# From unit 24 on: q, k and P turned in 32x32 blocks by VectorE, with a scratch in DRAM, in place of TensorE transposes

## The chip, the cores and the metric

The kernel runs on one core of a Trainium2 chip. The metric is the device time of one execution in microseconds (us), median of several runs. TensorE is PE (its weight loads PEld), VectorE DVE, ScalarE ACT, GpSimd POOL, SyncE SP; SP computes nothing here and issues all DMAs of the windowed path.

## The reference

Attention with 4 batches, 8 heads, 768 positions and head size 64, a local window of 96 keys, 8 global keys and a linear distance bias, then a feed-forward layer with a rational activation:

```python
scores = scale * np.matmul(q, k.transpose(0, 1, 3, 2))     # 4 x 8 x 768 x 768
keep = is_global | is_local                                # key < 8, or 0 <= row - key < 96
scores = np.where(keep, scores - slope * dist, -1e9)
a = softmax(scores)
x = np.matmul(a, v)        # laid out as 3072 tokens x 512
h = x @ w_in               # 512 -> 2048
g = (a0 + a1*h + a2*h**2 + a3*h**3) / (1 + |b0|*|h| + |b1|*h**2 + 1e-6)
out = g @ w_out            # 2048 -> 512, float32
```

## The kernel before, in words

Attention is cut into 96 units. A unit `u` is one pair of heads (4 pairs) in one tile of 128 rows (6 tiles in a batch, 24 in all): tile `u // 4`, pair `u % 4`. `unit(u)` also gives `i`, the tile's place in its batch. A tile with `i = 0` sees one block of keys, a later one its own block, the block before and the 8 global keys. The feed-forward is cut into 96 steps `f` (eight for each chunk of 256 tokens), each of 24 matmuls of 256 columns (`st_ffn1`, L312) and 12 of 512 columns (`st_ffn2`, L408), with the activation between them (`st_ew1`, `st_poly`, `st_sum`, `st_ew3`, `st_ew4`, `st_high`, `st_low`) on ACT, POOL and DVE. The weights and x are split in a high and a low part, so that three fast matmuls stand for one.

Units below 24 (`RAWQ`) work alone. From unit 24 on two units, here called a duo (`u` even and `u + 1`, four heads), are worked together, and four units (a tile) share one product P times v:

- `st_load` (L176): q and k of four heads come into `nat` (2 buffers).
- `st_split` (L482): a DMA copies `nat` to `sp`, typed for the fast matmul.
- `st_qkT` (L488): PE turns q and k of the duo, 4 transposes (L502) into PSUM (`tk`); `st_qkE` (L523): ACT copies them to `qT` (with the scale of the head) and `kT`.
- `st_score` (L558): scores in pieces of 32 queries, so that only the needed keys are computed; the key axis of a piece is ordered as a ring of 32-key blocks, own and previous block mixed (L580).
- `st_max`, `st_soft`, `st_total`, `st_norm` (L596 to L632): the masked maximum on DVE, the exponential on ACT, the scaling by the row's sum on POOL.
- `st_raw` (L634): a DMA copies P (`pr`) to `raws`, typed for the fast matmul (from unit 28).
- `st_pT` (L648): PE turns P, 2 transposes (L655) and for `i > 0` one for the global keys (L658); `st_pTE` (L664): DVE separates the ring into own and previous block by a multiplication with `block` (L676) and copies the global rows (L679).
- `st_pv` (L684): 16 matmuls for four units (L696), then `st_x` and `st_xl` split the result into the x of the feed-forward.

The order of the work has two parts. `LEAD` (L50) is a list of words that sets the order on all engines up to unit 29 (`T24` is `st_pT(24)`, `sp24` is `st_split(24)`, `BL` is `st_blocks`). Behind it a loop over `t` (L793) emits the steps, PE in that order; for ACT, DVE, POOL and SP a scheduler picks among the ready instructions by priority (`PRI`, L93), and the order so found is fixed in the program. At run time each engine takes its own instructions strictly in order and waits at each for its semaphores. The two halves of `st_ffn2(f)` come two loop steps behind `st_ffn1(f)`.

Of the kernel before, what the change touches and what calls it, by code (L numbers as in the profile page):

```python
# [17 lines left out]
P = 128  # L18
# [6 lines left out]
RAW = 28  # L25
RAWQ = 24
# [6 lines left out]
RAWS = 3  # L33
WK = P + 2 * G
PITCH = P + KB
# [57 lines left out]
PRI = dict(load=0, score=50, soft=100, ffn1a=150, qkT=200, pv=250, qkE=300, x=350, split=400, ew3=450, norm=500, raw=501,  # L93
# [51 lines left out]
def tile_kernel(ctx: ExitStack, tc: tile.TileContext, q, k, v, n_global, n_local,  # L145
# [336 lines left out]
    def st_split(u):  # L482
        if u >= RAWQ and u % 2 == 0:
            s = pl.att.tile([P, 2, 4, D], FR, tag="rawq", name=f"sp{u}", bufs=2)
            nc.sync.dma_start(out=s.bitcast(F32), in_=nat[u // 2])
            sp[u] = s

    def st_qkT(u):  # L488
        p = unit(u)[2]
        if u < RAWQ:  # L490
# [6 lines left out]
        elif u % 2 == 0:  # L497
            s = sp.pop(u)
            tk = pl.ps_t.tile([P, 2, 2, P], FR, tag="t", name=f"tk{u}")
            for y in range(2):  # L500
                for z in range(2):
                    nc.tensor.transpose(out=tk[:, y, z, :], in_=s[:, z, 2 * y:2 * y + 2].rearrange("p a d -> p (a d)"),  # L502
                                        identity=ident_r)
            tqk[u] = tk.bitcast(F32)


    def st_blocks():
        for p in range(NPAIR):
            for x in range(2):
                nc.gpsimd.memset(qsc[x * D:(x + 1) * D, p:p + 1], float(2.0 ** (2 * p + x - 2)))  # L510
        nc.gpsimd.tensor_copy(out=near[:, 0:G], in_=masks[:, 0, 0:G])
        nc.gpsimd.tensor_copy(out=near[:, G + P:], in_=masks[:, 0, 0:G])
        nc.gpsimd.tensor_copy(out=near[:, G:2 * G], in_=masks[:, 1, 0:G])
        nc.vector.tensor_tensor(out=near[:, 2 * G:G + P], in0=masks[:, 0, G:], in1=masks[:, 1, G:], op=ALU.max)
        nc.gpsimd.memset(raws2[:, :, :, G + P:].bitcast(F32), 0.0)
        nc.gpsimd.memset(block, 1.0)
        for w in range(2):
            sign = -1 if w else 1
            nc.gpsimd.affine_select(out=block[:, w, 0], in_=block[:, w, 0], pattern=[[sign * KB, P // KB], [0, KB]],
                                    base=-KB if w else KB - 1, channel_multiplier=-sign,  # L520
                                    compare_op=ALU.is_ge, fill=0.0)

    def st_qkE(u):  # L523
        c, t, p, b, i = unit(u)
        if u >= RAWQ:
            if u % 2 == 0:
                tk = tqk.pop(u)
                qTs[u] = qT = pl.att.tile([P, 2, P], F32, tag="qT", name=f"qT{u}")
                for y in range(2):
                    nc.scalar.activation(out=qT[:, y], in_=tk[:, y, 0], func=AF.Copy, scale=qsc[:, p + y:p + y + 1])  # L530
                nc.scalar.copy(out=kT[:, p:p + 2, i % 2, G:G + P], in_=tk[:, :, 1])
            return
# [11 lines left out]
    def st_kG(u):  # L544
        c, t, p, b, i = unit(u)
        if i:
            return
        if u < RAWQ:
            nc.gpsimd.tensor_copy(out=kG32[:, p, :], in_=k32[p][:, 0, 0:G])
        elif u % 2 == 0:  # L550
            for e in (0, G + P):
                nc.gpsimd.tensor_copy(out=kT[:, p:p + 2, :, e:e + G],
                                      in_=kT[:, p:p + 2, 0:1, G:2 * G].broadcast_to([P, 2, 2, G]))

    def first_of(x):
        return 0 if x else G

    def st_score(u):  # L558
        c, t, p, b, i = unit(u)
        if u < RAWQ:  # L560
# [9 lines left out]
        qT = qTs.pop(u)  # L570
        s_ps = [pl.ps_t.tile([P, 2, G + P], F32, tag="t", name=f"s{u}_{x}") for x in range(2)]
        for y in range(2):
            for part in range(2 if i else 1):
                for Q in range(P // KB - part):
                    for x in range(2):
                        first = first_of(x)
                        ends = (0, G + KB * (Q + 1) - first, G + P) if i else (G - first, G + P - first)
                        lo, hi = (0, G + P) if i and Q == P // KB - 1 else ends[part:part + 2]
                        own, qs = slice(x * D, (x + 1) * D), slice(Q * KB, (Q + 1) * KB)
                        nc.tensor.matmul(out=s_ps[x][qs, y, lo:hi], lhsT=qT[own, y, qs],  # L580
                                         rhs=kT[own, p + y, (i - part) % 2, first + lo:first + hi], start=True, stop=True)
# [3 lines left out]
    def st_kg(u):  # L585
        c, t, p, b, i = unit(u)
        if 1 <= i < NT - 1 and u < RAWQ:
            nc.gpsimd.tensor_copy(out=k32[p][:, i % 2, 0:G], in_=kG32[:, p, :])

    def cols_of(u, t, x):  # L590
        i = unit(u)[4]
        if u < RAWQ:
            return blocks_of(t, i)
        return t if i else t[:, G - first_of(x):][:, 0:P]

    def st_max(u):  # L596
        c, t, p, b, i = unit(u)
        s_ps = scores.pop(u)
        if u < RAWQ:
            mk = mask0 if i == 0 else masks[:, 0:2, :] if i % 2 else masks[:, 1:3, :]  # L600
            pr = pl.att.tile([P, 2, 2, P], F32, tag="prob", name=f"pr{u}")
        else:
            pr = pl.att.tile([P, 2 * PITCH], F32, tag="prob", name=f"pr{u}").rearrange("p (x w) -> p x w", x=2)[:, :, 0:G + P]
        st = stats[:, u % 4]
        for x in range(2):
            h = 2 * p + x
            if u >= RAWQ:
                mk = near[:, first_of(x):][:, 0:G + P] if i else mask0
            nc.vector.tensor_tensor_reduce(  # L609
                out=cols_of(u, pr[:, x], x), in0=cols_of(u, s_ps[:, x] if u < RAWQ else s_ps[x], x), in1=mk,  # L610
# [3 lines left out]
    def st_soft(u):  # L614
        pr, st = prob[u]
        for x in range(2):
            d = cols_of(u, pr[:, x], x)
# [9 lines left out]
    def st_norm(u):  # L627
        pr, st = prob[u]
        for x in range(2):
            d = cols_of(u, pr[:, x], x)  # L630
# [3 lines left out]
    def st_raw(u):  # L634
        if u < RAW:
            return
        pr = prob[u][0]
        raw = raws2[:, u % RAWS, :, 0:G + P]
        if unit(u)[4]:
            nc.sync.dma_start(out=raw.bitcast(F32), in_=pr)  # L640
        else:
            for x in range(2):
                nc.sync.dma_start(out=cols_of(u, raw[:, x].bitcast(F32), x), in_=cols_of(u, pr[:, x], x))
        prob[u] = (raw, None)
# [3 lines left out]
    def st_pT(u):  # L648
        i = unit(u)[4]
        pr, st = prob.pop(u)  # L650
        dt, eye = (FR, ident_r) if u >= RAW else (F32, ident)
        tps[u] = t_ps = pl.ps_t.tile([P, 2, 2, P] if u < RAWQ else [P, 3, P], dt, tag="t", name=f"tp{u}")
        if u >= RAWQ:
            for x in range(2):
                nc.tensor.transpose(out=t_ps[:, x], in_=pr[:, x, G - first_of(x):][:, 0:P], identity=eye)  # L655
            if i:
                ends = raws2[:, u % RAWS].rearrange("p x w -> p (x w)")[:, P:P + D]
                nc.tensor.transpose(out=t_ps[0:D, 2], in_=ends, identity=eye)  # L658
            return
        for x in range(2):  # L660
            for w in range(2 if i else 1):
                nc.tensor.transpose(out=t_ps[:, x, w, :], in_=pr[:, x, w, :], identity=eye)  # L662

    def st_pTE(u):  # L664
        i = unit(u)[4]
        pTs[u] = pT = pl.att.tile([P, 2, 2, P], F32, tag="pT", name=f"pT{u}", bufs=PTS)
        t_ps = tps.pop(u)
        t_ps = t_ps.bitcast(F32) if u >= RAW else t_ps
        copy = nc.scalar.copy if u < EARLY else nc.vector.tensor_copy
        if u < RAWQ:  # L670
# [361 lines left out]
```

## Time and profile before

| | us |
|---|---|
| median of 3 runs (lowest, highest) | 726.84 (724.93, 728.16) |
| the profiled execution | 725.79 |
| its span, first to last instruction | 723.8 |

| engine | busy, share of the span |
|---|---|
| PE | 700.3 us, 97% |
| DVE | 562.7 us, 78% |
| ACT | 552.7 us, 76% |
| POOL | 340.8 us, 47% |

The span is the time between the first and the last instruction in the trace; the execution's own time is 2.0 us longer. Busy times are unions of an engine's instructions. Matmuls overlap in the records, so what a matmul costs in a dense stretch is read from the start of one to the start of the next.

### The profile page before, as it was taken

Reading aid. Unit: us, or ns where it says so; the run is one execution under the profiler, and the core shown is the slowest. Engines: PE = TensorE matmul, PEld = TensorE weight load, DVE = VectorE, ACT = ScalarE, POOL = GpSimd, SP = SyncE. Lnnn points to the kernel's source line nnn. Section 1 sums busy time; section 2 is a strip of 40 time slices with the busy share of each in tenths; the row PEclk is TensorE's granted clock in tenths of the full one; section 3 lists DMA queues with packets and bytes.
Section 4 is the critical chain, followed back from the end, with each engine's and each line's share of the span. In section 5 each row is a group of like instructions: output and inputs, shape, how many; then the busy total and the mean of one; then the engine's idle time right before and its main releaser. Section 6 shows DMA issues by size and latency. Waiting matters only on the chain.

```text
span 723.8 us, 17630 instructions
## 1 busy us (share of the span) xinstructions
PE 700.3 (97%) x6515; PEld 602.1 (83%) x6515; DVE 562.7 (78%) x1419; ACT 552.7 (76%) x1302; POOL 340.8 (47%) x450
## 2 busy tenths in 40 slices
PE   5799999999999999999999999999999999999996
PEld 4577778768798888988888988888889888899995
DVE  6899999986976777877787877778687778777564
ACT  6899998867877867777776776877876867766774
POOL 2344646475445444455454454545445535444441
PEclk9999999999999999999999999999999999999998
DMA  8874446112322312323312322223222221100001
GB/s 196 254 223 128 147 140 174 39 44 74 99 67 76 98 54 81 100 62 89 104 47 77 104 62 77 92 73 89 89 61 77 90 62 54 54 19 1 30 1 35
DMA packets 110718, 62.29 MB, mean 86 GB/s; under 512 B 80672, under 2 KB 99616, under 8 KB 110624
## 3 DMA queue, kind: packets, MB, share of 16 engines
q1 hardware_dynamic: 110624, 61.07, 29.4%
q8 instruction: 54, 0.88, 0.5%
q14 instruction: 40, 0.33, 0.1%
HBM read 35.92 MB, written 6.29 MB: 58 GB/s over the span
## 4 chain that ended last, share of the span: by engine, by line
PE 85%; ACT 10%; DVE 2%; issue 1%; DMA 1%; SPq 1%; POOL 0%; ACTq 0%; POOLq 0%; DVEq 0%
PE acc L424 33%; PE h L330 32%; PE o L696 5%; PE s L580 3%; PE acc L420 3%; PE h L322 2%; ACT pr L618 2%; PE tk L502 2%; PE s L564 2%; PE tp L655 1%; DMA r<-in_moe_w_in_dram 1%; ACT qzero L537 1%; PE tp L662 1%; ACT r L261 1%; ACT fu L355 1%
## 5 line engine op out<-in xcount | busy, mean ns | idle before, releaser
L369 POOL TENSOR_TENSOR fa<-fa,fs 128x512 f32<-128x512 f32 (+1 forms) x86 | 110.3, 1282 | 234.4 <-ACT fs L357 226.9
L398 POOL TENSOR_TENSOR g<-fu,g 128x512 fp32r<-128x512 f32 x84 | 108.9, 1297 | 61.8 <-ACT g L395 54.8
L424 PE MATMUL acc<-wout_h,g 128*128 128x512 f32 x352 | 128.2, 408 | 0.7 <-POOL g L398 0.7
L355 ACT ACTIVATE fu<-h,coef 128x512 f32<-128x512 f32 x94 | 73.2, 778 | 69.7 <-PE h L330 69.5
L424 PE MATMUL acc<-h,g 128*128 128x512 f32 x336 | 121.4, 407 | 0.1
L385 DVE SCALAR_TENSOR_TENSOR fu<-fu,coef,q 128x512 f32<-128x512 f32 (+1 forms) x97 | 71.7, 739 | 57.8 <-ACT q L381 56.8
L330 PE MATMUL h<-xl,win_h 128*128 128x256 f32 x352 | 99.1, 282 | 0.7 <-DVE xl L735 0.6
L330 PE MATMUL h<-xh,win_h 128*128 128x256 f32 x352 | 99.6, 283 | 0.0
L330 PE MATMUL h<-xh,h 128*128 128x256 f32 x352 | 99.2, 282 | 0.0
L330 PE MATMUL h<-xl,h 128*128 128x256 f32 x352 | 98.2, 279 | 0.0
L395 ACT CAST g<-fu 128x512 fp32r<-128x512 f32 (+1 forms) x88 | 54.6, 620 | 49.1 <-DVE fu L387 49.0
L631 POOL TENSOR_SCALAR pr<-pr,stats 128x136 f32<-128x136 f32 (+2 forms) x170 | 65.9, 408 | 44.5 <-DVE stats L625 36.5
L380 ACT ACTIVATE fs<-fa,coef 128x512 f32<-128x512 f32 (+1 forms) x97 | 70.0, 722 | 21.3 <-POOL fa L369 19.8
L618 ACT ACTIVATE pr<-pr,stats 128x136 f32<-128x136 f32 (+2 forms) x192 | 80.5, 429 | 5.1 <-DVE stats L609 4.8
L364 DVE TENSOR_TENSOR fu<-fu,h 128x512 f32<-128x512 f32 (+1 forms) x97 | 65.8, 678 | 18.6 <-ACT fs L357 18.1
L424 PEld LDWEIGHTS acc<-wout_h,g 128*128 128x128 f32 x352 | 65.9, 188 | 15.2 <-issue 1.9
L424 PEld LDWEIGHTS acc<-h,g 128*128 128x128 f32 x336 | 62.9, 188 | 14.2 <-issue 1.7
L365 DVE SCALAR_TENSOR_TENSOR fu<-fu,coef,h 128x512 f32<-128x512 f32 (+1 forms) x97 | 71.8, 740 | 2.7
L386 DVE SCALAR_TENSOR_TENSOR q<-fa,coef,q 128x512 f32<-128x512 f32 (+1 forms) x97 | 72.2, 744 | 0.0
L330 PEld LDWEIGHTS h<-xl,win_h 128*128 128x128 f32 x352 | 66.2, 188 | 4.6 <-DVE xl L735 2.8
L387 DVE SCALAR_TENSOR_TENSOR fu<-q,fu 128x512 f32<-128x512 f32 (+1 forms) x97 | 66.5, 686 | 3.3
L330 PEld LDWEIGHTS h<-xh,win_h 128*128 128x128 f32 x352 | 66.2, 188 | 2.5 <-issue 0.5
(272 smaller groups left out, 1801.8 us busy)
## 6 DMA issues: line engine op xcount, KB each, us to landing
sp<-nat SPq DMA_DIRECT2D x36, 256.0 KB, 2.5
r<-in_moe_w_in_dram SPq DMA_DIRECT2D x16, 512.0 KB, 4.9
r<-in_moe_w_out_dram SPq DMA_DIRECT2D x16, 512.0 KB, 4.8
raws<-pr SPq DMA_DIRECT2D x60, 136.0 KB, 2.2
nat<-in_q_dram SPq DMA_DIRECT2D x48, 128.0 KB, 2.4
nat<-in_k_dram SPq DMA_DIRECT2D x48, 128.0 KB, 2.6
vt<-in_v_dram SPq DMA_DIRECT2D x48, 128.0 KB, 2.7
out_dram<-o SPq DMA_DIRECT2D x18, 256.0 KB, 2.2
```

The lines of the kernel that those rows point to most:

```text
L330: nc.tensor.matmul(out=h_of(f, y), lhsT=w[:, fs], rhs=x[:, ct, :], start=(n == 0), stop=(n == 3 * NCT - 1))
L355: nc.scalar.activation(out=u, in_=h, func=AF.Identity, scale=a3, bias=a2)
L365: nc.vector.scalar_tensor_tensor(out=u, in0=u, scalar=a1, in1=h, op0=ALU.add, op1=ALU.mult)
L369: side(f, SUM_V).tensor_tensor(out=a, in0=a, in1=s, op=ALU.add)
L380: nc.scalar.activation(out=s, in_=a, func=AF.Ln, bias=q1)
L385: nc.vector.scalar_tensor_tensor(out=u, in0=u, scalar=a0, in1=r, op0=ALU.add, op1=ALU.mult)
L386: nc.vector.scalar_tensor_tensor(out=r, in0=a, scalar=q1, in1=r, op0=ALU.add, op1=ALU.mult)
L387: nc.vector.scalar_tensor_tensor(out=u, in0=r, scalar=2.0, in1=u, op0=ALU.subtract, op1=ALU.mult, reverse0=True)
L398: side(f, G_V, f == NU - 1 and ys == 1).tensor_tensor(out=gs[f][:, 1, ys], in0=ew[f]["u"][:, ys], in1=gs[f][:, 0, ys], op=ALU.subtract)
L424: nc.tensor.matmul(out=acc, lhsT=gs[f][:, z, y, ts], rhs=w, start=(start and n == 0), stop=(stop and n == 2))
L618: nc.scalar.activation(out=d, in_=d, func=AF.Exp, scale=-1.0, bias=st[:, x:x + 1], accum_out=st[:, 2 + 2 * x:3 + 2 * x])
L631: (nc.vector if u < NORMS else nc.gpsimd).tensor_scalar(out=d, in0=d, scalar1=st[:, 6 + x:7 + x], scalar2=0.0, op0=ALU.mult, op1=ALU.add)
```

## The change

Transposes of q, k and P on PE are gone from unit 24 on. DVE's transpose turns each 32x32 block in place (rows of 32 partitions with 32 columns), which leaves a block in the partitions it came from. To bring the blocks into the partitions where the matmuls want them, SP writes the turned tile to a scratch in DRAM with one DMA per 32 partitions and reads it back with the rows in another order.

- q and k (`st_split`): POOL multiplies q by the scale of the head in place, DVE turns 128x512, four DMAs write `zq` (one scratch for each duo), one DMA (`st_gather`, new, word `sr`) reads it into `qk`, which takes the place of `qT` and `kT`.
- P: the four maps of a duo lie in one tile (`prob`); `st_pT` turns 128x640 (128x512 at `i = 0`) on DVE, 7 DMAs write own and previous blocks to `z` and one the global keys to `zg` (4 in all at `i = 0`); `st_pTE` reads them back with 3 DMAs (1 at `i = 0`) into `pT`, so the multiplication with `block` and the copies go.
- Scores: keys in whole blocks of 32, the 8 global keys in a block of their own that is mostly zeros, so a piece has 160 columns where it had 136.
- `st_raw`, the copies of `st_split` and `st_qkE` from unit 24, `block`, `raws2` and `kT` go. `st_blocks` clears `qk` (128x2560) on POOL and the two `z` by DMA.

```diff
     def st_split(u):
-        if u >= RAWQ and u % 2 == 0:
-            s = pl.att.tile([P, 2, 4, D], FR, tag="rawq", name=f"sp{u}", bufs=2)
-            nc.sync.dma_start(out=s.bitcast(F32), in_=nat[u // 2])
-            sp[u] = s
+        n = nat[u // 2]
+        nc.gpsimd.tensor_tensor(out=n[:, 0], in0=n[:, 0], in1=qsc[:, 2 * p:2 * p + 4].unsqueeze(2).broadcast_to([P, 4, D]),
+                                op=ALU.mult)
+        s = pl.att.tile([P, 4, 4, KB], F32, tag="rawq", name=f"sp{u}", bufs=2)
+        nc.vector.transpose(out=s.rearrange("p b z t -> p z b t"),
+                            in_=n.rearrange("p z (y x) (c d) -> p (z y) (x c) d", x=2, d=KB))
+        sp[u] = zq = pl.dram.tile([P, NB, P], F32, tag="zq", name=f"zq{u}", bufs=2)
+        for a in range(NB):
+            nc.sync.dma_start(out=zq[:, a].rearrange("(b d) f -> d b f", d=KB),
+                              in_=s[a * KB:(a + 1) * KB].rearrange("p b z t -> p b (z t)"))
+
+    def st_gather(u):
+        nc.sync.dma_start(out=qk[:, p // 2, i % 2, 0:NB].rearrange("p a z y t -> p (a z y t)"),
+                          in_=sp.pop(u).rearrange("p a f -> p (a f)"))
...
     def st_blocks():
-        nc.gpsimd.memset(raws2[:, :, :, G + P:].bitcast(F32), 0.0)
-        nc.gpsimd.memset(block, 1.0)
+        nc.gpsimd.memset(qk, 0.0)
+        for z in zs:
+            for w in range(2):
+                nc.sync.dma_start(out=z[w], in_=qk[:, 1, 1].rearrange("p a b c d -> p (a b c d)")[:, 0:NB * P])
...
     def st_score(u):
+                    ends = (Q + 1) % NB or NB + 1
+                    lo, hi = (0, NB) if i == 0 else (ends, NB + 1) if part else (0, ends)
...
+                        nc.tensor.matmul(out=s_ps[x][Q * KB:(Q + 1) * KB, y, lo * KB:hi * KB],
+                                         lhsT=qk[own, p // 2, i % 2, Q, 0, y, :],
+                                         rhs=qk[own, p // 2, (i - part) % 2, lo:hi, 1, y, :], start=True, stop=True)
...
     def st_pT(u):
+        n = NB + 1 if i else NB
+        s = pl.att.tile([P, NB + 1, 4, KB], F32, tag="raw", name=f"T{u}", bufs=2)
+        nc.vector.transpose(out=s[:, 0:n].rearrange("p b z t -> p z b t"),
+                            in_=prs[u // 2 % 2][:, :, 0:n * KB].rearrange("p z (b d) -> p z b d", d=KB))
+        flat = s.rearrange("p b z t -> p b (z t)")
+        tps[u] = z, zg = zs[u // 2 % 2], (pl.dram.tile([P, P], F32, tag="zg", name=f"zg{u}", bufs=2) if i else None)
+        for Q in range(NB):
+            rows = flat[Q * KB:(Q + 1) * KB]
+            for w, lo, hi in ((0, 0, Q + 1), (1, Q + 1, NB)):
+                if lo < hi and (i or w == 0):
+                    nc.sync.dma_start(out=z[w, lo * KB:hi * KB, Q * P:(Q + 1) * P].rearrange("(b d) f -> d b f", d=KB),
+                                      in_=rows[:, lo:hi])
+        if i:
+            nc.sync.dma_start(out=zg, in_=flat[:, NB])
 
     def st_pTE(u):
-            nc.vector.tensor_tensor(out=pT, in0=t_ps[:, 0:2].unsqueeze(1).broadcast_to([P, 2, 2, P]),
-                                    in1=block.broadcast_to([P, 2, 2, P]), op=ALU.mult)
-            for x in range(2):
-                copy(out=pT[0:G, 1, x, :], in_=t_ps[x * KB:x * KB + G, 2, :])
+        z, zg = tps.pop(u)
+        pT = held_pair(pts2, u, [P, 2, NB, 2, 2, KB], "pT")
+        flat = pT.rearrange("p w q y x t -> p w (q y x t)")
+        nc.sync.dma_start(out=flat[:, 0], in_=z[0])
+        if i:
+            nc.sync.dma_start(out=flat[KB:, 1], in_=z[1, KB:, :])
+            nc.sync.dma_start(out=pT[0:KB, 1].rearrange("p q y x t -> p q (y x t)"), in_=zg.rearrange("(q g) f -> g q f", g=KB))
...
-            if t:
-                on("split", t + 1, "sp")
+            on("split", t + 2, "sp")
+            on("gather", t + 1, "sr", "kG")
...
-            on("pT", t - 3, "T", "P")
-            if fixed and t % 2 == 0:
-                on("qkT", t, "qT")
-                on("qkE", t, "qE", "kG")
+                on("pT", t - 2, "T")
+                on("pT", t - 3, "P")
```

The order changes at three places that matter. On PE, between the two halves of one `st_ffn2` step (`acc_0` and `acc_1` are its two sums, `tp` the turned P, `tk` the turned q and k), before:

```order
L424 MATMUL acc_0_0_3119<-w_13l,g_3596 128x512
L424 MATMUL acc_0_0_3119<-h_6_1907,g_3596 128x512
L655 MATMUL tp_3747<-ident_r,raws_64 128x128 x2
L658 MATMUL tp_3747<-ident_r,raws_64 64x128
L502 MATMUL tk_3755<-ident_r,sp_3570 128x128 x4
L424 MATMUL acc_1_0_3143<-h_6_1907,g_3596 128x512
L424 MATMUL acc_1_0_3143<-w_12l,g_3596 128x512
```

and in the changed kernel:

```order
L421 MATMUL acc_0_0_3095<-h_6_1898,g_3538 128x512 x2
L421 MATMUL acc_0_0_3095<-w_13l,g_3538 128x512
L421 MATMUL acc_0_0_3095<-h_6_1898,g_3538 128x512
L421 MATMUL acc_1_0_3102<-h_6_1898,g_3538 128x512
L421 MATMUL acc_1_0_3102<-w_12l,g_3538 128x512
```

The transposes are gone and the two halves follow each other.

On SP, about a third into the work behind the lead (`vt` is v, `pT` the turned P that the product reads), before:

```order
L640 DMA raws_64<-pr_3440 128x2x136
L640 DMA raws_64<-pr_3443 128x2x136
L485 DMA sp_3783<-nat_3473 128x512
L181 DMA nat_3884<-in_q_dram 128x4x64
L182 DMA nat_3884<-in_k_dram 128x4x64
L707 DMA vt_2656<-in_v_dram 8x4x64
```

and in the changed kernel:

```order
L491 DMA zq_4404<-sp_4402 32x4x128
L657 DMA z_86<-T_3293 32x128
L657 DMA z_86<-T_3293 32x3x128
L657 DMA z_86<-T_3293 32x2x128 x2
L657 DMA z_86<-T_3293 32x3x128
L657 DMA z_86<-T_3293 32x128
L657 DMA z_86<-T_3293 32x4x128
L660 DMA zg_3295<-T_3293 128x128
L678 DMA pT_2240<-z_86 96x512
L676 DMA pT_2240<-z_86 128x512
L679 DMA pT_2240<-zg_3295 32x4x128
L491 DMA zq_4404<-sp_4402 32x4x128 x3
```

The reads of P (L676 to L679) stand directly behind the writes of the same P; and since each `zq` has its own scratch, loads and turns of q and k stand far ahead of their use: these four writes of `zq_4404` are for unit 54, around the P of unit 38. All the units' q and k are through when SP reaches the P of unit 56.

On POOL in the lead, at the word `BL` (`qsc` holds the scales, `nat_1276` is q and k of unit 24), before:

```order
L512 COPY near<-masks 128x8
L513 COPY near<-masks 128x8
L515 MEMSET raws_64 128x6x24
L516 MEMSET block 128x256
L519 AFFINE_SELECT block<-block 128x128 x2
L253 TENSOR_SCALAR w_12f<-r_12_1299 128x512
```

and in the changed kernel:

```order
L513 COPY near<-masks 128x8
L514 COPY near<-masks 128x8
L516 MEMSET qk 128x2560
L484 TENSOR_TENSOR nat_1276<-nat_1276,qsc 128x256
L250 TENSOR_SCALAR w_12f<-r_12_1292 128x512
```

A longer clearing and the scaling of q stand where the two selections stood; DVE's transpose of unit 24, which reads the scaled q, stands on DVE directly behind the operation on `near` (L514 before).

## Rows read from the trace of the kernel before

**Rows 1.** Stretches: us, busy us (instructions) PE PEld DVE ACT POOL, PEclk, DMA share, GB/s

```profile
0.00:50.00 50.00, 37.02 (x201) 28.21 (x201) 38.46 (x156) 41.25 (x131) 17.03 (x39) 1.00 0.80 226
200.00:600.00 400.00, 399.82 (x4322) 356.69 (x4321) 305.99 (x796) 298.67 (x712) 190.74 (x239) 1.00 0.27 78
```

**Rows 2.** The chain that ended last, shares of the span by engine

```profile
PE 85%; ACT 10%; DVE 2%; issue 1%; DMA 1%; SPq 1%; POOL 0%; ACTq 0%; POOLq 0%; DVEq 0%
```

**Rows 3.** PE's transposes by line: names, shapes, count | busy us, mean ns | idle before

```profile
L655 PE MATMUL tp<-ident_r,raws 128*128 128x128 f32 x136 | 19.6, 226 | 0.0
L502 PE MATMUL tk<-ident_r,sp 128*128 128x128 f32 x144 | 17.9, 247 | 1.5 <-PE s L580 1.0 <-DVE stats L609 0.5
```

**Rows 4.** Timeline, PE around the transposes of two units: start us, us, instruction

```profile
403.94 0.40 PE L424 MATMUL acc<-h,g 128*128 128x512 f32 x1
...
404.66 0.40 PE L424 MATMUL acc<-w_14l,g 128*128 128x512 f32 x1
...
409.55 0.39 PE L424 MATMUL acc<-w_1l,g 128*128 128x512 f32 x1
409.78 0.39 PE L424 MATMUL acc<-wout_h,g 128*128 128x512 f32 x1
410.01 0.29 PE L655 MATMUL tp<-ident_r,raws 128*128 128x128 f32 x2
...
410.84 0.40 PE L424 MATMUL acc<-w_0l,g 128*128 128x512 f32 x1
```

**Rows 5.** Timeline, PE's scores of a duo with i = 0 and of another

```profile
170.51 0.67 PE L580 MATMUL s<-kT,qT 64*32 64x128 f32 x32
171.11 0.50 PE L424 MATMUL acc<-h,g 128*128 128x512 f32 x1
...
401.91 0.84 PE L580 MATMUL s<-kT,qT 64*32 64x32 f32 x56
402.68 0.50 PE L424 MATMUL acc<-h,g 128*128 128x512 f32 x1
```

**Rows 6.** Timeline of the lead at `BL`: POOL, DVE, PE, with idle time before

```profile
115.96 0.32 POOL L516 MEMSET block<- 128x256 f32 x1
...
116.59 0.42 DVE L609 CUSTOM_DVE_ANT_0 pr<-s,masks 128x256 f32<-128x256 f32 x1 [1.03 <-PE s L564]
...
116.90 0.66 POOL L253 TENSOR_SCALAR w_12f<-r 128x512 f32<-128x512 f32 x1
...
123.10 0.89 PE L662 MATMUL tp<-ident,pr 128*128 128x128 f32 x4 [0.19 <-POOL pr L631]
```

**Rows 7.** Timeline, the last operation of a feed-forward step and its first reader

```profile
412.24 1.30 POOL L398 TENSOR_TENSOR g<-fu,g 128x512 fp32r<-128x512 f32 x1
...
417.58 0.50 PE L424 MATMUL acc<-wout_h,g 128*128 128x512 f32 x1
```

**Rows 8.** Timeline, SP's DMA issues: start us, us in issuing, tile

```profile
334.01 2.02 SPq L189 DMA_DIRECT2D vt<-in_v_dram  x4
...
388.71 0.30 SPq L707 DMA_DIRECT2D vt<-in_v_dram  x1
...
406.54 1.46 SPq L464 DMA_DIRECT2D out_dram<-o  x2
...
416.60 0.30 SPq L707 DMA_DIRECT2D vt<-in_v_dram  x1
...
417.92 0.37 SPq L189 DMA_DIRECT2D vt<-in_v_dram  x1
```

**Rows 9.** DMA issues: tiles, count, KB each, median us from issue to landing

```profile
r<-in_moe_w_in_dram SPq DMA_DIRECT2D x16, 512.0 KB, 4.9
...
nat<-in_q_dram SPq DMA_DIRECT2D x48, 128.0 KB, 2.4
```

**Rows 10.** DVE's work on P by line

```profile
L676 DVE TENSOR_TENSOR pT<-tp,block 128x512 f32<-128x512 f32 x60 | 41.2, 686 | 28.5 <-PE tp L658 28.0
L679 DVE COPY pT<-tp 8x128 f32<-8x128 f32 x104 | 28.8, 277 | 0.7
```

More of the change, by code (lines that the diff above doesn't have):

```diff
@@ L24 @@
 GBUFS = 3
-RAW = 28
-RAWQ = 24
+PAIRS = 24
 LAG = 12
@@ L90 @@
 """
-PRI = dict(load=0, score=50, soft=100, ffn1a=150, qkT=200, pv=250, qkE=300, x=350, split=400, ew3=450, norm=500, raw=501,
+PRI = dict(load=0, score=50, soft=100, ffn1a=150, qkT=200, pv=250, qkE=300, x=350, split=400, gather=420, ew3=450, norm=500, raw=501,
            ffn1b=550, ew1=600, ew4=650, ew2=700, ffn2a=750, pT=800, ffn2b=850, wsplit=990)
@@ L523, in st_qkE @@
     def st_qkE(u):
         c, t, p, b, i = unit(u)
[L525 to L531, printed above, removed]
+        if u >= PAIRS:
             return
@@ L569, in st_score @@
             return
-        qT = qTs.pop(u)
-        s_ps = [pl.ps_t.tile([P, 2, G + P], F32, tag="t", name=f"s{u}_{x}") for x in range(2)]
+        s_ps = [pl.ps_t.tile([P, 2, WK], F32, tag="t", name=f"s{u}_{x}") for x in range(2)]
         for y in range(2):
             for part in range(2 if i else 1):
-                for Q in range(P // KB - part):
+                for Q in range(NB - part):
+                    ends = (Q + 1) % NB or NB + 1
+                    lo, hi = (0, NB) if i == 0 else (ends, NB + 1) if part else (0, ends)
                     for x in range(2):
[L576 to L581, printed above, removed]
+                        own = slice(x * D, (x + 1) * D)
+                        nc.tensor.matmul(out=s_ps[x][Q * KB:(Q + 1) * KB, y, lo * KB:hi * KB],
+                                         lhsT=qk[own, p // 2, i % 2, Q, 0, y, :],
+                                         rhs=qk[own, p // 2, (i - part) % 2, lo:hi, 1, y, :], start=True, stop=True)
         for y in range(2):
@@ L602, in st_max @@
         else:
-            pr = pl.att.tile([P, 2 * PITCH], F32, tag="prob", name=f"pr{u}").rearrange("p (x w) -> p x w", x=2)[:, :, 0:G + P]
+            mk = near if i else mask0
+            pr = held_pair(prs, u, [P, 4, WK], "prob")[:, u % 2 * 2:u % 2 * 2 + 2]
         st = stats[:, u % 4]
@@ L629, in st_norm @@
         for x in range(2):
-            d = cols_of(u, pr[:, x], x)
+            d = cols_of(u, pr[:, x])
             (nc.vector if u < NORMS else nc.gpsimd).tensor_scalar(
                 out=d, in0=d, scalar1=st[:, 6 + x:7 + x], scalar2=0.0, op0=ALU.mult, op1=ALU.add)
[L634 to L644, printed above, removed]
     tps = {}
@@ L649, in st_pT @@
         i = unit(u)[4]
[L650 to L653, printed above, removed]
+        if u < PAIRS:
+            pr, st = prob.pop(u)
+            tps[u] = t_ps = pl.ps_t.tile([P, 2, 2, P], F32, tag="t", name=f"tp{u}")
             for x in range(2):
[L655 to L658, printed above, removed]
+                for w in range(2 if i else 1):
+                    nc.tensor.transpose(out=t_ps[:, x, w, :], in_=pr[:, x, w, :], identity=ident)
@@ new lines, in st_pTE @@
+        if u % 2:
+            return
+        z, zg = tps.pop(u)
[5 more added lines that the diff above has]
+            nc.sync.dma_start(out=pT[0:KB, 1].rearrange("p q y x t -> p q (y x t)"), in_=zg.rearrange("(q g) f -> g q f", g=KB))
+        pTs[u], pTs[u + 1] = (pT[:, :, :, y] for y in range(2))
@@ L972, in tile_kernel @@
     with ExitStack() as es:
+        pl.dram = es.enter_context(tc.tile_pool(name="dram", bufs=1, space=bass.MemoryType.DRAM))
+        zs[:] = [pl.dram.tile([2, P, NB * P], F32, tag=f"z{n}", name=f"z{n}", bufs=1) for n in range(2)]
         pl.ldp = es.enter_context(tc.tile_pool(name="ldp", bufs=2))
```

137 lines of the change are left out of this document (65 added, 72 removed).

## The prediction

> **What bounds the kernel now.** I read the stretches first, because they show whether one engine has no idle time where the change works: between 200 and 600 us PE is busy 399.82 of 400 us, DVE 305.99, ACT 298.67, POOL 190.74, and the granted clock is 1.00 (the upper level, 2.4 GHz) [rows 1]. The chain that ended last says the same of the whole span: 85% of it is PE [rows 2]. So a microsecond taken off PE there is a microsecond of the end, as long as no other engine or transfer becomes late, and the question is what SP, DVE and POOL get in its place. One round of the loop over a tile (two duos) takes 416.60 - 388.71 = 27.9 us, read from two loads of v that stand at the same place of it [rows 8]. The chip's time for the profiled execution is 725.8 us; my sum is made from that, and it lies 1.0 below the median of the runs.
>
> **PE loses the transposes.** The groups by line give 226 and 247 ns as means of overlapping records [rows 3], so I take the distance between starts instead. In a dense stretch two 512-column matmuls stand 409.78 - 409.55 = 0.23 us apart. With one unit's transposes of P between, two matmul places take 404.66 - 403.94 = 0.72 us, so these cost 0.72 - 2 x 0.23 = 0.26. With P, q and k they take 410.84 - 409.78 = 1.06, so 0.60 [rows 4]. A duo has one unit of each sort: 0.86 us. At `i = 0` the transpose of the global keys is absent in both, about 0.06 each, so 0.74. From unit 24 on there are 36 duos, 6 of them with `i = 0`: 30 x 0.86 + 6 x 0.74 = 30.2 us off PE, all in stretches where PE is the limit.
>
> **PE's scores get wider.** A piece has 160 columns instead of 136. From the two score rows, to the next matmul's start: 32 records with 2048 columns take 0.60 us, 56 records with 2176 columns 0.77 [rows 5]. The first is 0.29 ns for a column, but the records overlap on two halves of the array; a duo gets 384 more columns, and I take 0.2 ns for each, 0.08 us, since starts and weights, which don't change, are part of the row. 30 duos: +2.3 us. Bounds: nothing, if columns are hidden behind weight loads, and 0.77 x 24/136 x 30 = 4.1.
>
> **The lead.** At `BL`, POOL's clearing and the two selections took from 115.96 to 116.90 [rows 6]; now it clears ten times the 256 columns that took 0.32, which is 0.32 to 3.2 us, and I take 2.8, near proportional, because a start of an operation is a small part of such a row. Scaling q, 256 columns with two inputs, is half of the 1.30 us of a 512-column product [rows 7], 0.65. So POOL is 2.8 + 0.65 - 0.9 = 2.5 us later, and DVE, whose transpose of unit 24 waits behind it with the masked maxima of the lead queued, about 3.3, of which it had 1.03 idle. PE already waits 0.19 us for POOL soon after [rows 6], so this lateness reaches PE: +3 us (0 to 3.3). The clearing of `z` by DMA reads it but holds no engine.
>
> **DVE.** A tile's round has 305.99/400 x 27.9 = 21.3 us of DVE. It loses 4 x 0.686 + 8 x 0.277 = 5.0 [rows 10], and gets two turns of P (640 columns) and, while q and k run ahead, 4.8 turns of 512. No row shows such an instruction; the nearest, 512 columns in one pass, took 686 ns, so about 2 x 0.86 + 4.8 x 0.69 = 5.0. That is 21.3 of a round of 27.9 - 1.72 + 0.15 = 26.3 us: nothing is lost. At twice the price it would be 26.3, exactly full. POOL gets 4.8 x 0.65 on 13.3, also not bound; ACT only loses copies.
>
> By the Trainium skill's VectorE: DVE Perf Modes, "The three transpose paths", a 128x128 transpose is 311 ns on VectorE against 390 on TensorE, and its rules would leave a 128x128 one on TensorE. By 311 ns DVE's turns would be 9.1 us in a round, an estimate, still inside 26.3. The 390 isn't what these rows show in a dense stretch, where three transposes together took 0.26 us [rows 4].
>
> **SP, the term that decides.** The order has 786 DMAs on SP where it had 354. A duo's P now has 8 writes and 3 reads, q and k 4 writes and one gather. And they are uneven: q and k run ahead from unit 28 on and are through at the P of unit 56, so in six rounds of a tile (between the products of units 28 to 31 and 48 to 51) SP has 53 to 56 DMAs each, later 28 to 30, where it had 15 or 16. An issue costs SP (417.92 - 416.60)/3 = 0.44 us from start to start, or 2.02/4 = 0.505 back to back [rows 8]; I take 0.47, the middle, as both kinds of stretch occur: 55 x 0.47 = 25.9 us. To this come waits that hold everything behind them: the reads of P stand right behind the writes of the same P, and a load lands 2.4 us after its issue [rows 9], of which two issues pass meanwhile, so some 1.3 us twice a round; a little more traffic makes it 3.1 together. The chain load, scaling, turn, write of q and k (2.4 + 0.65 + 0.69 and the semaphores, some 5 us) lies beside the next duo's issues. So 29.0 us against 26.3 available: SP falls behind by 2.7 in each of six rounds, 16 us in all.
>
> Part is absorbed: the P reads stand a step of the loop (7 us) or more ahead of the product, and a feed-forward step has 417.58 - 413.54 = 4 us between POOL's last operation and PE's first use [rows 7], which covers DVE when it waits for a late load. I take 7 off once: +9 us. Bounds: at 0.44 and 2.6 us of waits a round takes 26.8, 0.5 over, six times 3: nothing lost. If writes to DRAM cost what the two stores of the output did, 1.46/2 = 0.73 [rows 8], 35 writes and 20 reads are 35.0, with waits 37.6: 11.3 x 6 - 7 = +61. I stay near the loads, since the new transfers are a quarter of a store's size.
>
> **Sum:** 725.8 - 30.2 + 2.3 + 3 + 9 = 709.9, **710 us**.
>
> **Rivals.** (a) *Transfers land late.* In the six rounds some 6 MB move in 26 us, about as much per us as in the first 50, where the DMA share was 0.80 at 226 GB/s [rows 1] and the loads of the weights landed after 4.9 us in the median [rows 9] (but with four times the size). With landings 0.8 us later, 3.2, the two waits for P cost 1.6 more and the 4.8 chains of q and k about 0.3 each, 1.4: a round is about 31.5, lateness 5.2 x 6 - 7 = 24, and the time 725: no change. For it: the share; against it: the small size of the transfers. The Trainium skill's DMA: Bandwidth & Descriptors, "Latency and other measured facts", gives HBM access as 0.2 us on average and 2 us at high load, the same direction; by its full 2 us it would be well on the slow side.
>
> (b) *SP becomes the bound, slower than before.* Writes at 0.65 instead of 0.47, between the loads and the stores: 35 x 0.65 + 20 x 0.47 = 32.2, with 2.6 of waits 34.8; 8.5 x 6 - 7 = 44, time 745. It decides from a round of 31.6 us on (lateness 25, all that the change wins), 0.53 us for each DMA at 2.6 us of waits. For it: the back-to-back row is at 0.505 already; against it: these issues are gone after unit 56.
>
> (c) *DVE's turns are slow.* At three times the price, 15 us, a round has 31.3 us of DVE while q and k run ahead: 5 x 6 less 7 is +23, and the time 724 without SP's 9 beside it. For it: the turn reads and writes 32-column pieces; against it: the product with `block` read PSUM and had two inputs.
>
> (d) *Nothing is late.* SP at the lower bound and the lead's wait hidden: 725.8 - 30.2 + 2 = 698.
>
> **How the numbers follow.** Forecast 0.45 (703 to 720), (a) 0.17, (b) 0.18, (c) 0.07, (d) 0.13. A measurement here tells 0.5% from no change: below 723.2 is faster, above 730.5 slower. The forecast and (d) are faster, with a small part of (a) and (c) 0.62; most of (a), half of (c) and little of (b) are within, 0.15; the rest of (b) and late ends of (a) and (c) 0.23. The range of 8 in 10 goes from (d) with the lead hidden, 695, to (b), 745.
>
> **What would show it.** PE: no rows of transposes behind unit 24, a round of about 26.3 us and no idle time after unit 56, where SP has 29 DMAs; if a round there is longer, the first term is wrong. Between about 180 and 350 us: rounds of 26.5 to 29 with PE's idle time released by DMA (product waits for P) or by POOL's `g` (feed-forward held behind a DVE turn that waits for q and k). No idle time there means (d); rounds over 31 mean (a) if SP mostly waits, (b) if SP mostly issues. DVE's turns above 1.5 us for 512 columns mean (c). At about 120 us PE should show 2 to 3 us of idle time after `BL`.

## The result and the profile after

| | before | changed |
|---|---|---|
| median, us | 725.88 (4 runs) | 735.83 (4 runs) |
| profiled execution, its span | 725.79, 723.8 | 734.78, 732.6 |
| PE busy in the span | 700.3 | 684.7 |
| PE idle in the span | 23.5 | 47.9 |

The changed kernel is slower: ratio 1.013, 95% interval 1.010 to 1.016. I forecast 710 and faster; 735.8 lies inside my range of 695 to 745, but on the slower side, which I gave 0.23.

Two stretches of the changed kernel: us, busy us (instructions) of PE, PEld, DVE, ACT, POOL, PE's granted clock, DMA share, GB/s:

```profile
200.00:400.00 200.00, 182.44 (x1823) 158.27 (x1815) 135.06 (x333) 121.19 (x269) 100.66 (x135) 0.96 0.65 168
400.00:600.00 200.00, 199.48 (x2125) 177.92 (x2124) 143.23 (x371) 145.65 (x328) 102.33 (x128) 1.00 0.39 107
```

Before, PE had next to no idle time in either (0.18 of 400 us) [rows 1]. Now 17.6 us are lost in the first half, where q and k run ahead, nearly nothing in the second, and the clock is lower in the first. PE's idle time, by what ended it (us in total, times, longest):

```profile
PE acc L421 <- POOL g L395: 8.3, 6, 2.9
PE s L566 <- DMA qk<-zq: 7.7, 2, 6.5
PE tp L641 <- DVE pr L629: 5.7, 5, 1.9
PE acc L421 <- ACT g L392: 4.0, 2, 3.1
PE h L327 <- DVE xl L736: 3.7, 5, 2.1
```

The third row is work of the lead, which waited for 4.6 us at the same place before. The second is two gathers there, 1.17 and 6.54 us. In the others, feed-forward and x come late, though neither ACT, DVE nor POOL is full. So the span's 8.8 us more are 24.4 more of idle time less 15.6 of busy time.

Where nothing waits, PE does what was forecast. The product of a tile, round after round, and a duo's scores with the next instruction:

```profile
437.38 0.44 PE L697 MATMUL o<-pT,vt 128*64 128x128 f32 x4
...
450.62 0.93 PE L566 MATMUL s<-qk 64*32 64x32 f32 x56
451.48 0.50 PE L421 MATMUL acc<-wout_h,g 128*128 128x512 f32 x1
...
463.67 0.55 PE L697 MATMUL o<-pT,vt 128*64 128x128 f32 x6
...
490.22 1.97 PE L697 MATMUL o<-pT,vt 128*64 128x128 f32 x32
```

Rounds of 26.3 and 26.5 us where one was 27.9 [rows 8]; scores of 0.86 us where they were 0.77 [rows 5].

How a wait comes about, at 340 to 348 us (SP, POOL, PE of the changed kernel):

```profile
338.89 1.29 POOL L366 TENSOR_TENSOR fa<-fa,fs 128x512 f32<-128x512 f32 x1
...
341.55 0.45 SPq L179 DMA_DIRECT2D nat<-in_q_dram  x1
342.04 0.53 SPq L180 DMA_DIRECT2D nat<-in_k_dram  x1
...
344.93 0.61 POOL L484 TENSOR_TENSOR nat<-nat,qsc 128x256 f32<-128x256 f32 x1 [4.75 <-ACT prob L616]
345.50 1.26 POOL L366 TENSOR_TENSOR fa<-fa,fs 128x512 f32<-128x512 f32 x1
346.72 1.27 POOL L395 TENSOR_TENSOR g<-fu,g 128x512 fp32r<-128x512 f32 x1
...
348.05 0.73 PE L421 MATMUL acc<-h,g 128*128 128x512 f32 x2 [2.87 <-POOL g L395]
```

POOL sits idle for 4.75 us ahead of a scaling of q (L484). The row names ACT, but the load of that q was issued only at 341.55, and 3.4 us later the scaling starts, so I read the load as what was waited for. The two feed-forward operations behind it wait too, and PE stops for 2.87 us. Over the run, ahead of the scaling and of DVE's turn of q and k (columns as in [rows 10]):

```profile
L484 POOL TENSOR_TENSOR nat<-nat,qsc 128x256 f32<-128x256 f32 x36 | 22.2, 618 | 72.5 <-DMA nat<-in_q_dram 34.4 <-issue 19.3 <-ACT o L454 6.5
L487 DVE STREAM_TRANSPOSE sp<-nat 128x512 f32<-128x512 f32 x36 | 25.4, 709 | 47.6 <-DMA zq<-sp 17.6 <-POOL nat L484 14.0 <-DMA z<-T 7.0
```

Why the loads come late is seen on SP, which is full in the run-ahead. The six rounds between the products that start at 200.16 and 382.70 us take 182.5 us, 30.4 each. SP issues 328 DMAs in them, and its waits add up to 16.8 us, none longer than 1.2; in the six rounds behind the run-ahead (410.82 to 568.18, 26.2 each) it issues 158 and waits for 80.1. PE itself waits for no DMA in the six rounds; these are all its waits there:

```profile
PE acc L421 <- POOL g L395: 6.5, 4, 2.9
PE acc L421 <- ACT g L392: 3.1, 1, 3.1
PE h L327 <- ACT xh L726: 2.8, 3, 1.4
PE h L327 <- DVE xl L736: 2.8, 3, 2.1
```

So late DMAs reach PE only by way of the other engines.

### The profile page after: what moved, and what is told of

Read it like the earlier page. It is cut to its first block, busy times and chain, and to the rows that moved or that the text cites. A ratio compares the mean times of both kernels' runs of the same rounds, so it can differ in the third digit from the quotient of the medians.

```text
span 732.6 us, 17209 instructions
## 1 busy us (share of the span) xinstructions
PE 684.7 (93%) x6167; PEld 585.6 (80%) x6167; DVE 536.7 (73%) x1320; ACT 520.4 (71%) x1173; POOL 359.2 (49%) x478
## 4 chain that ended last, share of the span: by engine, by line
PE 42%; ACT 4%; DMA 3%; SPq 2%; DVE 1%; POOL 1%; issue 0%; POOLq 0%; DVEq 0%
PE h L327 20%; PE acc L421 19%; DMA nat<-in_q_dram 2%; PE s L566 2%; PE o L697 1%; ACT prob L616 1%; ACT fs L377 1%; SPq L657 1%; DMA z<-T 1%; DVE xl L736 1%; ACT fu L352 1%; SPq L491 0%; DMA zq<-sp 0%; ACT g L392 0%; PE acc L430 0%
## 5 line engine op out<-in xcount | busy, mean ns | idle before, releaser
L421 PE MATMUL acc<-wout_h,g 128*128 128x512 f32 x352 | 121.5, 405 | 6.4 <-POOL g L395 5.4
L421 PE MATMUL acc<-h,g 128*128 128x512 f32 x336 | 114.8, 403 | 6.2 <-ACT g L392 3.1
L327 PE MATMUL h<-xl,win_h 128*128 128x256 f32 x352 | 100.8, 286 | 4.0 <-DVE xl L736 3.7
L327 PE MATMUL h<-xh,win_h 128*128 128x256 f32 x352 | 101.2, 288 | 3.0 <-ACT xh L726 2.8
L354 ACT ACTIVATE fs<-h,coef 128x512 f32<-128x512 f32 (+1 forms) x97 | 66.3, 683 | 2.8 <-DMA out_dram<-o 2.7
L327 PEld LDWEIGHTS h<-xh,h 128*128 128x128 f32 x352 | 66.1, 188 | 2.4 <-issue 0.8
L327 PEld LDWEIGHTS h<-xl,h 128*128 128x128 f32 x352 | 66.1, 188 | 2.1 <-issue 0.5
```

The source lines that it names most:

```text
L327: nc.tensor.matmul(out=h_of(f, y), lhsT=w[:, fs], rhs=x[:, ct, :], start=(n == 0), stop=(n == 3 * NCT - 1))
L354: nc.scalar.activation(out=s, in_=h, func=AF.Square, scale=b1)
L421: nc.tensor.matmul(out=acc, lhsT=gs[f][:, z, y, ts], rhs=w, start=(start and n == 0), stop=(stop and n == 2))
```

## The experiments

All times are medians beside runs of the kernel before on the same chip; idle time is that of the profiled execution (400 us less PE's busy time). The last column has the six rounds of the run-ahead: from the product that starts at 200.16 us in the changed kernel, and the same product in the others, to the sixth behind it, with PE's idle time in them. Before, they took 165.3 us (0.1).

| run | us | ratio to before (95%) | PE idle, 200 to 600 us | six rounds (PE idle) |
|---|---|---|---|---|
| changed kernel | 735.83 | 1.013 (1.010, 1.016) | 18.1 | 182.5 (15.5) |
| spread2 | 741.94 | 1.023 (1.018, 1.028) | 25.1 | 178.5 (13.1) |
| spread2_lead | 735.46 | 1.015 (1.011, 1.019) | 20.9 | 170.4 (9.5) |
| act_zq | 729.69 | 1.006 (1.004, 1.008) | 19.0 | 174.5 (11.3) |
| p_alone | 717.30 | 0.990 (0.989, 0.992) | 1.0 | 162.2 (0.4) |
| gate | 717.14 | 0.987 (0.984, 0.991) | 7.9 | 161.7 (2.3) |
| gate_lead | 714.12 | 0.983 (0.979, 0.987) | 5.3 | 161.2 (2.3) |
| gate2_lead | 711.77 | 0.980 (0.978, 0.982) | 3.7 | 160.2 (1.0) |
| pause | 768.62 | 1.059 (1.055, 1.063) | 24.2, two of the pauses | not compared |

**spread2: no run-ahead.**

```diff
...
-        sp[u] = zq = pl.dram.tile([P, NB, P], F32, tag="zq", name=f"zq{u}", bufs=2)
+        sp[u] = zq = zqs[u // 2 % len(zqs)]     # two tiles, made once, as z
...
```

> Only two scratch tensors for q and k instead of one for each duo, so SP cannot run ahead with q and k and has about 42 DMAs in each round of a tile instead of 55. Theory (in the six rounds of run-ahead SP's queue is full, DVE's turns of q and k wait for it with the feed-forward queued behind, and PE's idle time pulls its clock down): the 17 us of idle time between 200 and 400 us go, the granted clock there is back at 1.00, and the time is about 711 us (735.8 less 17 of idle time and 7 to 8 of clock). Rival (the way through DRAM is too long wherever it stands): the rounds stay near 29 to 30 us and the time at 730 or more.

Measured 741.9, slower than the changed kernel. The DMA share became even, and the waits spread with it:

```profile
200.00:400.00 200.00, 184.21 (x1888) 161.84 (x1889) 134.38 (x340) 125.56 (x281) 96.31 (x126) 0.95 0.54 143
400.00:600.00 200.00, 190.71 (x1975) 167.58 (x1975) 139.24 (x348) 135.80 (x299) 102.82 (x132) 0.99 0.49 131
```

PE now loses 9.3 us behind 400 us too, where the changed kernel lost 0.5. So time is lost without a full SP too: in the six rounds SP issues 258 DMAs here instead of 328 and its waits add up to 51.7 us. Where turns of q and k are, time is lost. But a full SP is not ruled out as the reason in the changed kernel, and I took it as fallen too soon: with two scratch tensors SP's writes of `zq` wait for the gather of the duo two before (52.2 us in 22 times, 3.6 at most), the loads behind them on SP with them. That wait is new here, and POOL's idle time ahead of the scaling grows from 72.5 to 84.7 us:

```profile
L486 POOL TENSOR_TENSOR nat<-nat,qsc 128x256 f32<-128x256 f32 x36 | 22.3, 620 | 84.7 <-DMA nat<-in_q_dram 45.6 <-ACT prob L618 11.7 <-DVE stats L623 10.7
```

**spread2_lead: the gather of unit 30 earlier.** In the lead `T24 sr28` became `T24 sp30 sr28`, and `n28 sp30` became `n28 sr30`.

> As spread2, and in the lead the turn of q and k of unit 30 stands some 8 us earlier and its gather follows directly. Theory for the lead: PE's 6.5 us of idle time near 195 us is a gather that was started too late, not the longer clearing at BL; it goes, with the low clock behind it, and the time is 7 to 10 us below that of spread2. Rival (the lead is late because of POOL's clearing): the same time as spread2 within 2 us.

735.5, 6.5 below spread2, just short of the 7 to 10 that I expected. The wait of 6.5 us went, but the gather of unit 28 now came 3.3 us late and a product 4.4, so a part only moved.

**act_zq: part of SP's issues on ACT.** `nc.sync.dma_start` became `nc.scalar.dma_start` for the writes of `zq`.

> The changed kernel with the four writes of each zq issued by ACT instead of SP; the run-ahead stays. SP has 36 DMAs in a round of the run-ahead instead of 55. Theory (SP's issuing is what is full): idle time between 200 and 400 us falls from 17 to under 6, time 712 to 720. Rival (landing times or DVE's order are the limit, not SP's issuing): 730 to 738.

729.7, just outside the rival's range and far from the theory's. PE idles 18.5 us between 200 and 400 us, as much as with all issues on SP, but that stretch holds other work here. The profiled execution (735.25 us, the longest of four from 728.21 on) is 10 us behind in the lead: the product that starts at 200.16 us in the changed kernel starts at 210.34. The six rounds from there on take 174.5 us instead of 182.5, with 11.3 us of PE's idle time instead of 15.5, SP's waits in them add up to 65.8 us instead of 16.8, and the time ahead of the scaling falls from 72.5 to 34.6, as I read it because loads stand behind fewer writes. So SP's full queue has a part in it, some 8 us in this execution, but with the queue no longer full most of PE's waits are left.

**p_alone: q and k by PE again.** `st_split`, the transposes of `st_qkT` and the words of q and k in the order are those of before; ACT copies into `qk` (of the longer edit, the copies of q):

```diff
...
+                for y in range(2):
+                    nc.scalar.activation(out=own[:, :, 0, y], in_=tk[:, y, 0].rearrange("p (a t) -> p a t", t=KB), func=AF.Copy,
+                                         scale=qsc[:, p + y:p + y + 1])
...
```

> Only P is turned by DVE and through DRAM; q and k of each duo are turned by PE again and copied by ACT. SP has about 32 DMAs in a round. Theory: no idle time beyond that of before, PE is rid of the transposes of P, about 18 us, and pays 2 for the wider scores: about 710 us. Rival (the P's way through DRAM itself delays the products): idle time of PE released by the product's wait, and 725 us or more.

717.3, 7.7 below before where 16 were expected, with 399.04 of 400 us busy. P's way through DRAM makes no wait in the loop: there a DMA is waited for by SP and PE, far ahead of need, while POOL and DVE, but for one wait of 1.7 us, wait for compute alone. Its rounds take 27.0 us in the mean where they took 27.6 (six rounds, in the table), 0.5 less each, where the sum's terms for P and the scores give 0.9: P's part of the gain is smaller than I had taken.

**gate: the same DMAs, but no operation stands where it waits for one.**

```diff
+        if u >= FIXED and u % 2 == 0 and u + 4 < NU:          # in st_max
+            p = unit(u + 4)[2]
+            gates[u + 4] = g = pl.att.tile([P, 4], F32, tag="qg", name=f"qg{u + 4}", bufs=2)
+            nc.vector.scalar_tensor_tensor(out=g, in0=st[:, 0:1].broadcast_to([P, 4]), scalar=st[:, 0:1],
+                                           in1=qsc[:, 2 * p:2 * p + 4], op0=ALU.is_equal, op1=ALU.mult)
...
-        in1=qsc[:, 2 * p:2 * p + 4].unsqueeze(2).broadcast_to([P, 4, D]),     # in st_split
+        in1=gates.pop(u, qsc[:, 2 * p:2 * p + 4]).unsqueeze(2).broadcast_to([P, 4, D]),
```

> The first theory (too many DMAs on SP in the run-ahead) fell: with two scratch tensors the run-ahead was gone and the time rose. Second theory: POOL's scaling and DVE's turn of q and k stand in the order right where the scheduler thinks that their load or their buffer is there; it comes later, and the feed-forward operations queued behind on the same engine wait with them. Here the scaling of a duo gets its factors from an operation of 4 columns on DVE behind the maximum of the duo two before, so that both stand a whole duo or more behind their load. All DMAs and all other work stay. Expected by this theory: no waits of POOL and DVE for loads or zq from 200 us on, rounds of 26.3 to 26.6, PE's idle time from 210 to 700 us under 3 us, time 709 to 713 (the lead's late gather stays). Rival (issuing and landing of the DMAs themselves are too slow): rounds of 28 or more, time over 722.

717.1, 18.7 below the changed kernel. The rows of the scaling and the turn, and the stretch to set beside those of spread2:

```profile
L485 POOL TENSOR_TENSOR nat<-nat,qg 128x256 f32<-128x256 f32 x31 | 19.0, 614 | 0.2 <-POOL g L396 0.2
...
L488 DVE STREAM_TRANSPOSE sp<-nat 128x512 f32<-128x512 f32 x36 | 25.5, 710 | 22.5 <-POOL nat L485 19.5 <-DMA vt<-in_v_dram 3.0
```

```profile
200.00:400.00 200.00, 194.42 (x2062) 171.75 (x2063) 151.52 (x380) 135.95 (x305) 103.67 (x135) 0.98 0.55 145
400.00:600.00 200.00, 197.72 (x2090) 175.09 (x2089) 154.30 (x383) 142.81 (x318) 106.87 (x137) 1.00 0.52 139
```

The DMA share and the GB/s are about those of spread2, but POOL's 84.7 us ahead of the scaling there (72.5 in the changed kernel) are 0.2, and PE's idle time between 200 and 600 us is 7.9 instead of 25.1. So this much of the cause is shown: PE loses its time where instructions at the head of POOL's and DVE's queues wait for DMAs that come late; as many DMAs without these waits cost little. It isn't shown by the step from the changed kernel alone, because the gate also ends the run-ahead: in the six rounds SP issues 240 DMAs instead of 328. Of the 20.9 us by which these rounds get shorter (182.5 to 161.7), 8 go in act_zq, too, where SP is no longer full; the rest goes only here, where POOL and DVE hardly wait for DMAs either. No run has a full SP without these waits, so how the two divide stays open. The time is 4 us above what I expected, as PE waits 0.7 to 0.9 us for `xl` in every other round, so that rounds of 26.3 and 27.3 us alternate.

**gate_lead: gate and the earlier gather.**

> As gate, and the turn and gather of unit 30 earlier in the lead. The wait of 6.5 us for the gather near 195 us goes; by the second theory 702 to 706. Rival (the lead's wait only moves to the next thing that SP brings): 708 to 712.

714.1. The 6.7 us went; 3.1 for the gather of unit 28 and 2.2 for a product came instead, so the wait moved, as the rival says. The time is above both ranges, and the intervals of gate and gate_lead overlap.

**pause: what an idle PE costs.** The kernel before, with this in `st_high`:

```diff
...
+        if f in (40, 56, 72) and not pl.split:
+            for _ in range(16):
+                nc.scalar.copy(out=ew[f]["u"][:, ys], in_=ew[f]["u"][:, ys])
...
```

> The kernel before with 16 added copies in place on ACT ahead of one cast of g in each of three feed-forward steps (40, 56, 72), so that PE waits there while no DMA and nothing on PE is added. It asks what an idle stretch of PE costs. If the lower granted clock in the changed kernel (0.93 to 0.95 between 200 and 350 us) follows from PE's idle time, the clock falls behind each pause here too, and the time grows by clearly more than the idle time added, by 1.2 to 1.6 times that. Rival (the clock has another cause, such as the DMA traffic): the clock stays at 1.00 and the time grows by the idle time alone.

768.6: 43.5 us more, for three idle stretches of 11.95, 11.79 and 11.79 = 35.5. PE after the first, and the clock (third figure from the end) around it:

```profile
365.02 0.79 PE L427 MATMUL acc<-wout_h,g 128*128 128x512 f32 x1 [11.95 <-ACT g L398]
```

```profile
352.00:354.00 2.00, 1.07 (x10) 0.87 (x8) 0.41 (x1) 2.00 (x6) 0.40 (x2) 1.00 0.72 255
356.00:358.00 2.00, 0.00 (x0) 0.00 (x0) 1.43 (x2) 1.94 (x4) 1.27 (x1) 0.60 0.00 0
364.00:366.00 2.00, 0.98 (x2) 0.50 (x2) 0.00 (x0) 1.97 (x4) 0.96 (x1) 0.50 0.00 0
368.00:370.00 2.00, 2.00 (x11) 1.60 (x10) 0.42 (x1) 0.80 (x3) 0.78 (x1) 0.50 0.00 0
372.00:374.00 2.00, 2.00 (x34) 1.87 (x40) 0.00 (x0) 0.05 (x1) 0.00 (x0) 1.00 0.54 124
```

The clock falls to 0.50 (1.2 instead of 2.4 GHz) while PE is idle, stays there for some 5 us of work behind the pause, and a pause costs (43.5 - 35.5)/3 = 2.7 us beyond itself; 2.1 of them are PE's own slower work (706.5 us busy instead of 700.3). The changed kernel shows it around its longest gap, 192.24 to 198.78, with no pause built in:

```profile
194.00:196.00 2.00, 0.00 (x0) 0.00 (x0) 1.18 (x2) 1.48 (x3) 0.36 (x1) 1.00 0.80 229
198.00:200.00 2.00, 1.22 (x56) 1.07 (x56) 1.38 (x3) 0.67 (x2) 1.27 (x1) 0.50 1.05 261
202.00:204.00 2.00, 2.00 (x8) 1.62 (x7) 1.15 (x10) 2.00 (x9) 1.12 (x2) 0.68 0.29 72
```

The Trainium skill's TensorE: Matmul & The Clock Gate, "What's actually happening", has a gate with these two levels that goes by how busy the engine was; the rows agree. The growth over the idle time alone, 1.23 times, is at the low end of what I expected.

**gate2_lead: the gate behind the turn of P.** As gate_lead, with the operation of 4 columns in `st_pT`, for the duo three later, and `sr28 sp30` in the lead.

> As gate_lead, but the factors of a duo come behind the turn of P of the duo three before, so that the scaling and the turn stand behind the subtraction that makes the low part of x and no longer ahead of it; and in the lead the turn of unit 30 stands behind the gather of unit 28. If the 0.67 to 0.95 us that PE waits in every other round of gate_lead for that subtraction come from the place of the turn on DVE, they go (6 us with nine waits) and the lead's wait for the gather of unit 28 falls from 3.1 to about 1.2: 705 to 709. Rival (DVE is too full there wherever the turn stands): within 2 us of gate_lead's 714.

711.8, the best version: 0.980 of before (0.978 to 0.982) and 24 us below the changed kernel. PE is busy for 396.29 of 400 us. The nine waits for `xl` are three, and the gather of unit 28 is 1.4 us late; some feed-forward waits near 335, 484 and 496 us came instead, hence 3 us above my range, and 2 below gate_lead, so just outside the rival's too.

This run also shows that POOL's idle time is not by itself what costs. It is nearly that of the changed kernel again:

```profile
L485 POOL TENSOR_TENSOR nat<-nat,qg 128x256 f32<-128x256 f32 x33 | 20.3, 616 | 68.3 <-DVE qg L655 64.0 <-issue 4.1
L488 DVE STREAM_TRANSPOSE sp<-nat 128x512 f32<-128x512 f32 x36 | 25.4, 707 | 18.9 <-POOL nat L485 18.7
```

But these are 28 waits of at most 3.3 us for an operation of DVE and one of 4.1, where nine of the changed kernel's waits at this place lie between 3.9 and 9.0. The prediction read 4 us as what a feed-forward step has to spare [rows 7]; waits below it hardly reach PE.

## Why the prediction was wrong

- **The transposes.** Right in kind, too large in size. Behind the run-ahead rounds of 27.7 to 27.9 us became 26.3 to 26.6, 1.4 less where the sum had 1.6. Over the run PE's busy time fell by 20.9 us (700.3 to 679.4 in gate2_lead, at about the mean clock of before), where 30.2 - 2.3 = 27.9 were forecast. Why the lead and the end gave less than the rounds is open.
- **The scores.** Right: 0.09 us more for a duo; the sum had 0.08.
- **The lead.** Prices right, conclusion wrong. The clearing took 2.23 us (2.8 in the sum), the scaling 0.61 (0.65), and DVE waited 2.11 us at its turn, but PE hardly noticed: it was busy 48.30 of the 50 us from 100 on, and 49.05 before, with 1.07 us of idle time at 119.94 where I expected 2 to 3.

```profile
114.28 2.23 POOL L516 MEMSET qk<- 128x2560 f32 x1
116.47 0.61 POOL L484 TENSOR_TENSOR nat<-nat,qsc 128x256 f32<-128x256 f32 x1
...
117.12 0.71 DVE L487 STREAM_TRANSPOSE sp<-nat 128x512 f32<-128x512 f32 x1 [2.11 <-POOL nat L484]
```

The lead did lose time, elsewhere: 6.54 us at the gather of unit 30. Its turn stands in the last line of the list, and SP had other DMAs between:

```profile
188.60 1.77 SPq L491 DMA_DIRECT2D zq<-sp  x4
...
194.96 0.62 SPq L498 DMA_DIRECT2D qk<-zq  x1
...
198.78 1.45 PE L566 MATMUL s<-qk 64*32 64x32 f32 x56 [6.54 <-DMA qk<-zq]
```

The prediction's lead term has no gather in it.

- **DVE.** Right: turns of 709 ns and 816 ns in the mean (0.69 and 0.86 in the sum), DVE far from full. The turns of a round come to 5.0 us, as in the sum; the 9.1 by 311 ns was too much. Rival (c) is out.
- **SP.** Right up to the last step. SP was full in the six rounds, as forecast, and a round took 54.7 DMAs x 0.505 + 2.8 us of waits = 30.4 us, where the sum had 55 x 0.47 + 3.1 = 29.0 (from 328 DMAs, 182.5 us and 16.8 us of waits). What failed is the step that takes 7 us off and leaves +9: that "the chain load, scaling, turn, write of q and k ... lies beside the next duo's issues", and that 4 us of slack "covers DVE when it waits for a late load", once. The six rounds came out 182.5 - 157.4 = 25 us longer than the six behind them, the slower clock included; nothing was absorbed. I counted these waits on SP, as delay of the DMAs. They stand on POOL and DVE, whose queues carry the feed-forward: at each such turn everything behind it waits for a load or for a write to land, up to 5.0 us on POOL (a load of q) and 4.8 on DVE (a write of `zq`), and so more than the slack. The prediction names such a hold among its signs ("feed-forward held behind a DVE turn that waits for q and k"), but gives it no term. Removing these waits and the run-ahead together is worth 19 us (gate against the changed kernel), removing the waits at nearly the same DMA share 25 (gate against spread2, which has SP's new waits besides).
- **The clock.** Absent from the sum: I read 1.00 in both stretches of [rows 1] and let idle time cost itself alone. PE is busy 684.7 us here and 679.4 in gate2_lead, with the same 6167 instructions: some 5 us of slower work.

So the span's +8.8 us come out as about -21 of PE's work (700.3 - 679.4), +24 of idle time, and +5 of clock. The sum had -28, +12 (3 for the lead, 9 for SP) and nothing: of the 25 us between 710 and 735, 7 are PE's work, 12 idle time and 5 the clock. Rival (b) was nearest: SP did become the bound of the six rounds and mostly issued, though at 30.4 us a round, short of the 31.6 at which it was to take all that the change wins; the other losses of the list came on top. Rival (a) is not what happened: q's loads landed after 2.4 us in the median, as before [rows 9].

What stays open: how much of the cost is SP's full queue and how much the place of the turns, since the gate takes both away at once; how much is POOL's wait and how much DVE's (in gate2_lead POOL's sum stays at 68.3 us and DVE's falls from 47.6 to 18.9, but POOL's waits are shorter, too); and what put act_zq's profiled execution 10 us behind in the lead.

## What to carry to other kernels

When work moves from a queue that only waits (SP) or from the bound engine to an engine that is "half idle", ask of each moved instruction what it waits for, and what stands behind it in the same order: idle time of an engine is only free if nothing needed soon is queued behind the wait, or if each wait, not their sum, is shorter than what those can spare. A scheduler that places an instruction that reads a DMA's result as soon as it thinks that the DMA is done holds up everything behind it when the DMA lands later; tie it to a compute event a step behind the landing. Then count the issues of each round on the queue that issues the DMAs: a full one makes the loads late in the first place. And price idle time of TensorE with the slower clock behind it.

## What the runs showed of the hardware

- A DVE transpose of 512 float32 columns in 32x32 blocks takes 709 ns, of 640 columns 839 ns: little more than a plain operation on 512 columns (686 ns in [rows 10]).
- The operation of 4 columns in gate, right behind a maximum whose result it reads, had a mean of 598 ns; in gate2_lead, behind a turn, 251 ns:

```profile
L614 DVE SCALAR_TENSOR_TENSOR qg<-stats,qsc 128x4 f32<-128x4 f32 x31 | 18.5, 598 | 0.0
```

Why it varies was not tried.
